# Logarithms of the softmax sums folded into T's rows; the heads' shares applied by ScalarE at O; new step orders

## Chip, cores and metric

One of the eight cores of a Trainium2 chip runs the kernel. The metric is the device time in microseconds. Before the change the median of three runs is 2738.21 us (2737.31 to 2740.78).

## What is computed

A transformer block on 2048 tokens of width 1024. A condition vector gives shifts, scales and gates (`mod`); then a layer norm, attention with 32 heads of width 32 in four segments of 512 tokens, an output projection, a second layer norm and a GEGLU feed-forward of width 3584. In each segment, attention mixes a local softmax with what a memory matrix recalls of the earlier segments:

```python
logits = jnp.einsum("bhqd,bhkd->bhqk", qs, ks) * scale + mask
p = _softmax(logits, axis=-1)
a_dot = jnp.einsum("bhqk,bhkd->bhqd", p, vs)
num = jnp.einsum("bhld,bhde->bhle", pq, M)
den = jnp.einsum("bhld,bhd->bhl", pq, z)[..., None] + 1e-6
a_mem = num / den
o = g * a_mem + (1.0 - g) * a_dot
```

`g` is a sigmoid of `beta`, one number a head.

## The kernel before

All matrix products run on TensorE (PE) with operands split into a high and a low part, three products for one. After an opening (modulation, first layer norm, first projections) comes attention, then the output projection, then the feed-forward by products of half-size blocks.

**Steps.** Attention runs in 32 steps (line 1414): two halves of the sequence, in each eight groups of four heads (g), for each group two segments (s). The loop at line 1605 has three steps in hand: in its turn n the *values* of step n-1 are made, the *scores* of step n, and the *projections* of step n+1. Below, "step n" is turn n of this loop. What a turn does is cut into short pieces with names, and `ORDER` (lines 1415 to 1465) writes out by hand, for each turn, in which order they are issued; every engine and the DMA queue of SyncE (SP) take their instructions strictly in that order. The pieces that matter:

- S0 to S3 (`rows`, line 530): scores with queries as rows. PE makes one S tile a head; VectorE (DVE, line 542) adds the mask and takes the row's maximum with reversed sign into `mm`; ScalarE (ACT, line 544) takes the exponential, and its accumulator gives the row's sum `ll`.
- tm (`maxima`, line 547): DVE splits the maxima into two parts and transposes them in 32x32 blocks. tq (`to_queries`, line 557): DVE writes them into rows 96 to 127 of the query tile `qs`, so that the product T comes out with the maximum subtracted.
- tr (`shares`, line 563): one over the sums, times 1-g (`omg`), on DVE; ACT spreads the factors over 32 columns a head.
- T0 to T3 (line 626): scores again, keys as rows, from the extended queries; ACT takes the exponential (line 633), GpSimd (POOL) masks it (line 634). P0 and P2 (line 638): the products with the values, into the one PSUM tile O.
- rt (`factors`, line 652): PE transposes the spread factors in four blocks into a PSUM tile R (line 649), ACT copies it out. rm (line 656): DVE multiplies O by it. yt (line 659): PE transposes the recalled part Y, DVE adds it. zs stores the result.
- nu, dn, mz: the memory's part; A: this segment's sum for the memory, product M. K0 to K7 and o0, o1 (kn on ACT, vx on DVE): projections to keys and values; kt: keys turned (product kT), copied as kh and kl; dk: three DMAs spread them into `ks`. Q0 to Q3, qo, ea, eb, dq: the same for the queries.
- G, C, D, l, L, m: the next group's weights, fetched, cut on ACT and subtracted on POOL. wl and wd: a row of the modulation, loaded and multiplied on DVE. ns, nc, n, nl: the layer norm of later segments. x, wo, wp, ga: operands of the output projection.

PSUM tiles for S, T, R, Y, M, kT and nu come from one pool of five, taken in turn (`s_ps`, line 99). `sj`, the scores' scratch, has three buffers. The opening (line 1478) sets `omg` at line 1517.

Of the kernel before, what the change touches and what calls it, by code (L numbers as in the profile page):

```python
# [36 lines left out]
def block_kernel(ctx: ExitStack, tc: tile.TileContext, x, c, wmod, wq, wkv, wo, beta, wg, wu, wd, out):  # L37
# [487 lines left out]
    def scores(u, n, g, s):  # L525
# [4 lines left out]
        def rows(i):  # L530
# [7 lines left out]
            for j in range(4):  # L538
# [81 lines left out]
    def values(u, n, g, s):  # L620

        nm = f"{g}_{s}"
        qs, ks, vx = ST[n][:3]
        d, pts = {}, {}

        def T(kc):
            n = L - kc * P
            nn = n
            for j in range(4):
                ps = s_ps(f"T{nm}_{j}{kc}")  # L630
                nc.tensor.matmul(ps[:, :nn], ks[:, j, kc * P:(kc + 1) * P], qs[:, j, L - nn:], start=True, stop=True)  # L631
# [13 lines left out]

        def turned(r, name):
            ps = s_ps(name + nm)
            for i in range(4):
                nc.tensor.transpose(ps[:, i * P:(i + 1) * P], r[:, i].rearrange("p a b -> p (a b)"), ident)  # L649
            return ps  # L650

        def factors():
            d["r"] = tmp_tile("R" + nm)
            nc.scalar.activation(d["r"], turned(SC[n][0], "R"), AF.Copy)

        def scaled():
            nc.vector.tensor_mul(d["r"], d["o"], d["r"])

        def recalled():
            nc.vector.tensor_add(d["r"], d["r"], turned(SY[n], "Y"))  # L660

        for kc in range(4):
            u[f"T{kc}"] = lambda kc=kc: T(kc)
        u["P0"] = lambda: PV(0)
        u["P2"] = lambda: PV(2)
        u["rt"] = factors
        u["rm"] = scaled
        if s > 0:
            u["yt"] = recalled
        u["zs"] = lambda: nc.sync.dma_start(oT_d[g * P:(g + 1) * P, s * L:(s + 1) * L], d["r"])  # L670
# [147 lines left out]
    def feed_forward():  # L818
# [562 lines left out]
        for m in range(NCH):  # L1381
# [96 lines left out]
    def opening():  # L1478
# [244 lines left out]
```

## Time and profile before

| | us |
|---|---|
| median of three runs | 2738.21 |
| the profiled execution | 2737.69 |
| its span, first to last instruction | 2735.9 |
| PE busy | 2710.2 |
| DVE busy | 1553.0 |
| ACT busy | 1202.4 |
| POOL busy | 850.2 |

PE's busy time is nearly the span. A matmul's end is modelled and successive matmuls overlap, so busy time alone doesn't tell whether PE ran at its best: a matmul held back for less than the length of its neighbours shows as a longer distance between starts. In the timeline, rows that repeat are merged: "x4" is four instructions, the first number is the start of the first, the second the time to the end of the last.

### The profile page before, as it was taken

What the parts mean: (1) busy time and instruction counts of PE and PEld (TensorE: products, weight loads), DVE (VectorE), ACT (ScalarE), POOL (GpSimd) and SP (SyncE); (2) the same over time, 40 slices, a digit from 0 to 9 for tenths busy, and PEclk for the clock granted to TensorE, in tenths of its full rate; (3) what the DMA queues carried; (4) which work ended last, traced back from release to release, by engine and by line L of the source; (5) the groups of instructions that cost most, each with busy time, mean ns of one, the idle gap of its engine ahead of it and who ended that gap; (6) DMA issues with size and microseconds to landing.
All of it is one profiled execution on the core that took longest, in us unless ns stands there. A gap on an engine that the chain in (4) does not pass through costs nothing.

```text
span 2735.9 us, 43050 instructions
## 1 busy us (share of the span) xinstructions
PE 2710.2 (99%) x14748; PEld 2279.8 (83%) x14748; DVE 1553.0 (57%) x3516; ACT 1202.4 (44%) x2811; POOL 850.2 (31%) x1446
## 2 busy tenths in 40 slices
PE   7999999999999999999999999999999999999999
PEld 6888888888888888888888888888888888888887
DVE  7777667676777735555555455343433254475456
ACT  6777777667767634343333233111111133233323
POOL 4333334433333434254445451443531000000000
PEclk9999999999999999999999999999999999999999
DMA  7454545444443569788898778999998687795563
GB/s 262 132 147 137 139 122 152 117 117 143 115 129 102 163 211 304 238 300 326 311 351 313 262 276 279 363 359 352 367 353 314 219 316 250 264 306 198 184 207 124
DMA packets 244891, 637.78 MB, mean 233 GB/s; under 512 B 24768, under 2 KB 49344, under 8 KB 244672
## 3 DMA queue, kind: packets, MB, share of 16 engines
q1 hardware_dynamic: 244672, 635.03, 68.2%
q8 instruction: 117, 1.92, 0.3%
q14 instruction: 102, 0.84, 0.1%
HBM read 372.79 MB, written 211.81 MB: 214 GB/s over the span
## 4 chain that ended last, share of the span: by engine, by line
PE 96%; DMA 2%; DVE 1%; issue 0%; ACT 0%; SPq 0%; DVEq 0%; ACTq 0%
PE f L1139 39%; PE y L1353 19%; PE kv L383 12%; PE q L389 6%; PE y L714 5%; PE S L540 3%; PE T L631 3%; PE O L643 3%; PE num L599 1%; PE M L582 1%; PE kv L512 1%; PE tpb L266 1%; PE kT L417 1%; PE R L649 0%; PE Y L649 0%; DMA wm_d<-wmod 0%
## 5 line engine op out<-in xcount | busy, mean ns | idle before, releaser
L1139 PE MATMUL f<-A,B 128*128 128x512 f32 x4704 | 1072.7, 390 | 0.0
L1139 PEld LDWEIGHTS f<-A,B 128*128 128x128 f32 x4704 | 881.4, 188 | 184.4 <-issue 1.0
L1353 PE MATMUL y<-B,L 128*128 128x512 f32 x2352 | 533.3, 389 | 0.0
L1353 PEld LDWEIGHTS y<-B,L 128*128 128x128 f32 x2352 | 441.4, 188 | 91.7
L544 ACT ACTIVATE sj<-sj,mm 128x384 f32<-128x384 f32 (+3 forms) x512 | 281.3, 553 | 49.0 <-DVE mm L542 48.7
L542 DVE CUSTOM_DVE_ANT_0 sj<-S,mask 128x384 f32<-128x384 f32 (+3 forms) x512 | 228.0, 488 | 105.5 <-PE S L540 86.1
L634 POOL TENSOR_SCALAR_AFFINE_SELECT pt<-pt 128x128 f32<-128x128 f32 x512 | 164.1, 343 | 290.0 <-ACT pt L633 283.5
L853 ACT ACTIVATE L<-X 128x512 fp32r<-128x512 f32 x168 | 105.8, 630 | 257.8 <-PE y L1353 166.8
L633 ACT ACTIVATE pt<-T 128x256 f32<-128x256 f32 (+3 forms) x512 | 181.9, 445 | 66.5 <-PE T L631 63.6
L383 PE MATMUL kv<-w,hhh 128*128 128x256 f32 x1024 | 200.3, 286 | 0.0
L855 DVE TENSOR_TENSOR L<-X,L 128x512 fp32r<-128x512 f32 x168 | 115.8, 690 | 146.9 <-ACT L L853 146.7
L1173 ACT ACTIVATE g<-g 128x512 f32<-128x512 f32 x56 | 35.4, 631 | 369.7 <-DVE g L1172 369.7
L374 POOL TENSOR_TENSOR w<-r,w 128x256 fp32r<-128x256 f32 x180 | 134.0, 776 | 158.2 <-ACT w L368 158.1
L383 PE MATMUL kv<-w,hha 128*128 128x256 f32 x896 | 177.2, 285 | 1.9 <-DVE vx L401 1.9
L1078 POOL TENSOR_TENSOR rw<-rw,gbb 128x256 f32<-128x256 f32 x112 | 91.2, 847 | 249.9 <-DMA rw<-wd 167.3
L383 PEld LDWEIGHTS kv<-w,hhh 128*128 128x128 f32 x1024 | 164.8, 191 | 1.4 <-issue 0.4
L383 PEld LDWEIGHTS kv<-w,hha 128*128 128x128 f32 x896 | 144.9, 190 | 4.0 <-DVE vx L401 2.2
L383 PE MATMUL kv<-w,hlh 128*128 128x256 f32 x512 | 144.7, 283 | 0.0
L383 PE MATMUL kv<-w,hla 128*128 128x256 f32 x448 | 126.6, 282 | 0.0
L714 PE MATMUL y<-wo,hho 128*128 128x512 f32 x384 | 126.0, 394 | 0.4 <-DVE xr L718 0.4
L1160 ACT ACTIVATE g<-f 128x512 f32<-128x512 f32 x56 | 33.5, 598 | 206.7 <-PE f L1139 206.7
L1150 ACT ACTIVATE c<-f 128x512 f32<-128x512 f32 x56 | 33.4, 597 | 172.6 <-PE f L1139 172.6
(244 smaller groups left out, 4212.4 us busy)
## 6 DMA issues: line engine op xcount, KB each, us to landing
bc_d<-B SPq DMA_DIRECT2D x189, 512.0 KB, 5.3
B<-bc_d SPq DMA_DIRECT2D x189, 512.0 KB, 5.4
B<-wc_d SPq DMA_DIRECT2D x112, 512.0 KB, 3.7
hid_d<-g SPq DMA_DIRECT2D x56, 512.0 KB, 4.7
wc_d<-T SPq DMA_DIRECT2D x56, 512.0 KB, 7.1
X<-hid_d SPq DMA_DIRECT2D x112, 256.0 KB, 4.7
wr<-gd_d SPq DMA_DIRECT2D x84, 256.0 KB, 4.1
qs<-qh SPq DMA_DIRECT2D x64, 256.0 KB, 3.6
```

Source lines behind the costliest of these rows:

```text
L374: nc.gpsimd.tensor_sub(w[:, 1, c], r[:, c], f32(w[:, 0, c]))
L383: nc.tensor.matmul(ps, b[:, sl], w[:, a], start=(kt == 0 and a == 0 and b is hi), stop=(kt == KT - 1 and a == 1), **kw)
L389: nc.tensor.matmul(ps, w[:, a], b, start=(kt == 0 and a == 0 and b is hi), stop=(kt == KT - 1 and a == 1), **kw)
L542: nc.vector.tensor_tensor_reduce(out=sj[:, :nv], in0=ps[:, :nv], in1=mask[:, L - nv:], scale=-1.0, scalar=3.4e38, op0=ALU.add, op1=ALU.min ...
L544: nc.scalar.activation(sj[:, :nv], sj[:, :nv], AF.Exp, bias=mm[:, j, i:i + 1], scale=-1.0, accum_out=ll[:, i, j:j + 1])
L633: nc.scalar.activation(pt, ps[:, nn - n:nn], AF.Exp)
L634: nc.gpsimd.affine_select(pt[:, :P], pt[:, :P], pattern=[[1, P]], compare_op=ALU.is_ge, fill=0.0, base=0, channel_multiplier=-1)
L714: nc.tensor.matmul(ps, b[:, i * P:(i + 1) * P], w[:, a, g % 2], start=(g == 0 and a == 0 and b is hi), stop=(g == G - 1 and a == 1))
L853: nc.scalar.activation(hi, src, AF.Copy)
L855: eng.tensor_sub(lo[:, k], src[:, k], f32(hi)[:, k])
L1139: nc.tensor.matmul(ps, B[m, i][:, a, kt * P:(kt + 1) * P], A[p, i, kt][b], start=(start and kt == 0 and a == 0 and b == 0), stop=(kt == 3 ...
L1353: nc.tensor.matmul(banks[t], ops[k][:, y, t * P:(t + 1) * P], B[slots[k]][:, x], start=(i not in (2, 4, 3) and j == 0 and x == 0 and y == ...
```

## The change

The row's exponential is divided by its sum in the exponent: the logarithm of the sum is subtracted from the reversed maximum before that goes into the query tile, so that T's exponential gives shares that sum to one. The factors are therefore neither spread, nor transposed, nor multiplied in. tr is now the logarithm on ACT, and stands ahead of tm in every step. 1-g is a column for each group (`omc`), with which ACT scales O at rm. The table set that holds exponential and logarithm is named at the start. rt is gone from all orders, and the orders are written anew. Core of the diff (of the orders, those of which the prediction speaks):

```diff
+    nc.scalar.preload_act_table_set("natural_log_exp_and_others")
...
-    omg = pa.tile([P, H], F32, name="omg")
+    omc = pa.tile([P, G], F32, name="omc")
...
+        def logs():
+            d["ln"] = t2("ln" + nm, "rc", bufs=2, shape=(P, 4, 4))
+            nc.scalar.activation(d["ln"], d["ll"], AF.Ln)
+
         def maxima():
             mm = d["mm"]
+            nc.vector.tensor_sub(mm, mm, d["ln"].rearrange("p i j -> p j i"))
...
-        def shares():
-            rc = t2("rc" + nm, "rc", bufs=2, shape=(P, 4, 4))
-            nc.vector.reciprocal(rc, d["ll"])
-            nc.vector.tensor_mul(rc, rc, omg[:, 4 * g:4 * g + 4].unsqueeze(1).to_broadcast([P, 4, 4]))
-            rx = t2("rx" + nm, "rx", shape=(P, 4, 4, DH))
-            nc.scalar.activation(rx, rc.unsqueeze(3).to_broadcast([P, 4, 4, DH]), AF.Copy)
-            SC[n] = [rx, None]
...
-        u["tr"] = shares
+        u["tr"] = logs
...
-        def factors():
+        def scaled():
             d["r"] = tmp_tile("R" + nm)
-            nc.scalar.activation(d["r"], turned(SC[n][0], "R"), AF.Copy)
-
-        def scaled():
-            nc.vector.tensor_mul(d["r"], d["o"], d["r"])
+            nc.scalar.activation(d["r"], d["o"], AF.Identity, scale=omc[:, g:g + 1])
...
-        u["rt"] = factors
...
         (0,):
-            "N K K N G1 K N N G2 K G0 K S0 S1 C1 S2 K S3 C2 K l1 l2 A tm tr tq L1 K K L2 K",
+            "N K K N G1 K N N G2 K G0 K S0 S1 C1 S2 K S3 C2 K l1 l2 A tr tm tq L1 K K L2 K",
...
         (2, 4, 6, 8):
-            "G1 Q0 T0 wd Q1 T1 Q2 P0 ns nc T2 Q3 T3 qo G2 n0 rt P2 K0 ea eb S0 C1 K1 dq S1 K2 S2 l1 K3 n1 K4 "
-            "nl C2 S3 L1 rm l2 K5 tm G0 wl K6 o0 K7 nd o1 ne tr A tq yt kt dk L2 ek zs",
+            "wd Q0 G2 Q1 Q2 T0 ns Q3 T1 P0 nc T2 A T3 qo n0 K0 nd S0 K1 ea C2 S1 G1 eb dq K2 S2 K3 C1 n1 l2 K4 l1 S3 K5 "
+            "P2 nl o0 L2 tr tm K6 tq rm L1 K7 yt G0 wl o1 kt dk ek zs ne",
...
         (14,):
-            "K0 K1 K2 T0 K3 T1 wd o0 x P0 x T2 S0 x G1 x K4 S1 C1 G2 x A l1 Q0 x S2 L1 Q1 x Q2 S3 x x K5 tm "
-            "T3 Q3 K6 tq K7 qo x P2 o1 C2 l2 rt tr rm G0 yt L2 x x kt ek dq ea dk x zs eb x",
+            "K0 x K1 x Q0 T0 K2 G2 wd T1 K3 S0 wd x x x x P0 o0 x x C2 S1 x l2 Q1 G1 K4 L2 wd Q2 x T2 S2 x x T3 Q3 qo x "
+            "K5 C1 S3 x ea A wd l1 L1 G0 eb K6 dq x K7 P2 o1 tr rm tm kt tq yt ek x dk x x zs x x",
...
         (17,):
-            "D0 K0 K1 K2 mz m0 K3 m1 o0 T0 K4 T1 K5 S0 Q0 S1 K6 S2 P0 T2 Q1 S3 Q2 tm Q3 T3 K7 tq qo P2 o1 rt "
-            "rm yt nu dn dq kt dk tr wl ek ea zs eb",
+            "K0 D0 m0 K1 m1 K2 T0 K3 T1 P0 T2 o0 Q0 T3 wl S0 S1 Q1 S2 Q2 Q3 qo S3 K4 K5 ea K6 K7 P2 mz eb o1 tr rm tm kt "
+            "tq dq yt dk nu dn ek zs",
         (18, 20, 22, 24, 26, 28):
-            "G2 G0 K0 K1 K2 T0 K3 T1 G1 o0 rt P0 T2 Q0 T3 S0 Q1 S1 mz wd Q2 Q3 qo C1 K4 C2 S2 K5 S3 P2 rm l1 "
-            "dq ea yt zs eb K6 K7 A tm nu l2 o1 kt tr ek wl dk tq L1 L2 dn",
+            "K0 G2 K1 K2 T0 mz K3 G1 o0 T1 K4 S0 C2 Q0 S1 P0 S2 Q1 T2 G0 Q2 Q3 wd T3 qo C1 K5 S3 K6 l1 A K7 P2 o1 tr dq "
+            "tm kt L1 rm yt wl ek tq l2 nu dn dk ea eb L2 zs",
         (19, 21, 23, 25, 27):
-            "mz wd D0 K0 K1 K2 m0 m1 K3 o0 T0 K4 T1 Q0 S0 K5 S1 Q1 rt S2 P0 S3 Q2 T2 tm K6 Q3 T3 wl tq qo K7 "
-            "P2 rm o1 nu ea kt yt tr dq dn dk zs wd ek wl eb",
+            "K0 D0 K1 K2 m0 T0 K3 o0 wl T1 K4 S0 Q0 S1 P0 mz m1 wd wd T2 wl Q1 T3 S2 Q2 Q3 qo K5 S3 K6 dq K7 P2 o1 tr tm "
+            "kt tq rm yt nu dk dn ek zs ea eb",
         (29,):
-            "K0 ga K1 D0 mz K2 m0 K3 T0 Q0 wl o0 T1 S0 Q1 S1 P0 S2 K4 S3 tm m1 wo K5 Q2 tq T2 wo Q3 T3 K6 qo "
-            "P2 rt ea eb K7 tr dq rm yt o1 nu dn kt ga dk zs ek",
+            "K0 D0 K1 m0 wd K2 T0 K3 o0 ga T1 K4 S0 K5 wo mz S1 P0 S2 m1 Q0 ga S3 Q1 tr wo tm Q2 T2 Q3 T3 K6 P2 K7 qo ea "
+            "nu tq rm dq o1 yt dn kt eb dk ek wl zs",
...
         (31,):
-            "mz K0 Q0 K1 T0 K2 T1 rt x P0 T2 T3 wp S0 K P2 S1 K K3 K4 S2 Q1 rm K5 S3 tm K6 Q2 tq nu yt K7 Q3 zs tr "
-            "dn",
+            "mz K0 Q0 T0 K1 T1 wp P0 T2 Q1 T3 Q2 S0 K2 K3 P2 S1 K4 rm S2 yt K5 K S3 K K6 tr tm tq nu dn K7 Q3 zs",
...
-        nc.vector.tensor_scalar(omg, gall, -1.0, 1.0, op0=ALU.mult, op1=ALU.add)
+        for j in range(4):
+            q = slice(DH * j, DH * (j + 1))
+            nc.vector.tensor_scalar(omc[q], gall[q].rearrange("p (g j) -> p g j", j=4)[:, :, j], -1.0, 1.0,
+                                    op0=ALU.mult, op1=ALU.add)
```

## Rows read from the trace of the kernel before

**Rows 1.** The page: busy time, share of the span and instructions of each engine.
```profile
PE 2710.2 (99%) x14748; PEld 2279.8 (83%) x14748; DVE 1553.0 (57%) x3516; ACT 1202.4 (44%) x2811; POOL 850.2 (31%) x1446
```

**Rows 2.** Table by stretch, attention: us, busy time, granted clock, DMA share, GB/s.
```profile
80.97:976.00 895.03, 894.01 (x6569) 776.28 (x6568) 621.98 (x2036) 648.10 (x1843) 336.49 (x772) 1.00 0.47 134
```

**Rows 3.** PE's timeline, steps 14, 18, 19, 29: start us, us, engine, line, tiles.
```profile
451.10 2.68 PE L643 MATMUL O<-pt,vx 128*32 128x512 f32 x16
...
563.83 0.86 PE L631 MATMUL T<-qs,ks 128*128 128x384 f32 x4
564.53 0.60 PE L649 MATMUL R<-ident,rx 128*128 128x128 f32 x4
565.06 2.09 PE L643 MATMUL O<-pt,vx 128*32 128x512 f32 x16
...
569.41 0.92 PE L540 MATMUL S<-ks,qs 96*128 96x128 f32 x4
...
596.00 0.56 PE L540 MATMUL S<-ks,qs 96*128 96x128 f32 x4
...
599.75 0.60 PE L649 MATMUL R<-ident,rx 128*128 128x128 f32 x4
600.11 0.95 PE L540 MATMUL S<-ks,qs 96*128 96x384 f32 x4
600.98 1.71 PE L643 MATMUL O<-pt,vx 128*32 128x512 f32 x16
...
873.55 1.36 PE L540 MATMUL S<-ks,qs 96*128 96x128 f32 x4
```

**Rows 4.** Timeline of all engines, end of step 18 to the next T0.
```profile
578.39 1.09 PE L540 MATMUL S<-ks,qs 96*128 96x512 f32 x4
...
583.03 0.19 ACT L544 ACTIVATION_READ_ACCUMULATOR sj<-sj,mm 128x1 f32 x1
...
584.88 0.17 DVE L550 CAST mt<-mm 128x16 fp32r<-128x16 f32 x1
...
585.29 0.86 DVE L555 STREAM_TRANSPOSE tt<-mt 32x32 f32<-32x32 f32 x4
...
587.74 1.70 DVE L559 TENSOR_SCALAR qs<-tt,seli 32x512 fp32r<-32x512 f32 x4
...
591.56 0.63 PE L631 MATMUL T<-qs,ks 128*128 128x512 f32 x2
```

**Rows 5.** Instruction groups by shape, ACT and DVE: xcount | busy us, mean ns | idle.
```profile
L654 ACT ACTIVATE R<-R 128x512 f32<-128x512 f32 x32 | 19.9, 623 | 8.4 <-PE R L649 8.4
...
L334 ACT ACTIVATE h<-tpa,modT 128x512 f32<-128x512 f32 x16 | 12.1, 769 | 6.2 <-DVE modT L171 2.3 <-POOL hla L345 2.3 <-PE tpa L327 1.4
...
L127 ACT ACT_TABLE_LOAD x1 | 1.3, 1283 | 0.8 <-PEq L1716 0.8
L1160 ACT ACT_TABLE_LOAD x1 | 1.3, 1283 | 0.0
...
L127 ACT ACTIVATE gall<-bb 128x32 f32<-128x32 f32 x1 | 0.2, 229 | 1.8 <-DMA bb<-beta 1.8
...
L657 DVE TENSOR_TENSOR R<-O,R 128x512 f32<-128x512 f32 x32 | 21.9, 686 | 3.3 <-PE O L643 2.8 <-ACT R L654 0.4
```

**Rows 6.** DVE's timeline in the opening; idle time and its releaser in brackets.
```profile
8.84 0.69 DVE L232 BATCH_NORM_STATS2 sta<-x 128x6 f32<-128x512 f32 x1 [0.74 <-DMA x<-x]
```

**Rows 7.** The chain of waits, in order of time: start us, us, what.
```profile
585.97 5.75 PE kv L383 x48
```

**Rows 8.** DVE's timeline, end of step 0.
```profile
75.83 3.09 DVE L559 TENSOR_SCALAR qs<-tt,seli 32x512 fp32r<-32x512 f32 x4
```

**Rows 9.** Timelines of ACT and POOL behind T1 of step 18.
```profile
564.26 1.64 ACT L633 ACTIVATE pt<-T 128x384 f32<-128x384 f32 x4 [0.23 <-PE T L631]
...
564.82 1.44 POOL L634 TENSOR_SCALAR_AFFINE_SELECT pt<-pt 128x128 f32<-128x128 f32 x4 [0.43 <-ACT pt L633]
```

**Rows 10.** The page, DMA issues: xcount, KB each, median us from issue to landing.
```profile
qs<-qh SPq DMA_DIRECT2D x64, 256.0 KB, 3.6
```

More of the change, by code (lines that the diff above doesn't have):

```diff
@@ L348, in norm_seg @@
             yield
-    hT, W, Mst, ST, SC, SY, PK = {}, {}, {}, {}, {}, {}, {}
+    hT, W, Mst, ST, SY, PK = {}, {}, {}, {}, {}, {}
     ks_t = []
@@ L1416, in block_kernel @@
         (0,):
-            "N K K N G1 K N N G2 K G0 K S0 S1 C1 S2 K S3 C2 K l1 l2 A tm tr tq L1 K K L2 K",
+            "N K K N G1 K N N G2 K G0 K S0 S1 C1 S2 K S3 C2 K l1 l2 A tr tm tq L1 K K L2 K",
         (1,):
-            "K0 T0 K1 D0 ns K2 T1 rt nc P0 mz m0 nu dn K3 T2 n0 n1 o0 Q0 Q1 T3 nd S0 ne nl m1 P2 S1 rm S2 K4 "
-            "Q2 S3 yt tm Q3 K5 K6 K7 tq wl qo o1 zs tr dq A kt ea eb dk ek",
+            "T0 K0 mz K1 T1 A P0 T2 ns K2 K3 nc D0 T3 n0 K4 nd n1 o0 K5 S0 m0 Q0 S1 K6 S2 m1 Q1 S3 Q2 Q3 nu dn ne nl K7 "
@@ L1421, in block_kernel @@
+            "qo tr P2 o1 rm ea tm tq kt dq dk yt eb zs ek",
         (2, 4, 6, 8):
-            "G1 Q0 T0 wd Q1 T1 Q2 P0 ns nc T2 Q3 T3 qo G2 n0 rt P2 K0 ea eb S0 C1 K1 dq S1 K2 S2 l1 K3 n1 K4 "
-            "nl C2 S3 L1 rm l2 K5 tm G0 wl K6 o0 K7 nd o1 ne tr A tq yt kt dk L2 ek zs",
+            "wd Q0 G2 Q1 Q2 T0 ns Q3 T1 P0 nc T2 A T3 qo n0 K0 nd S0 K1 ea C2 S1 G1 eb dq K2 S2 K3 C1 n1 l2 K4 l1 S3 K5 "
+            "P2 nl o0 L2 tr tm K6 tq rm L1 K7 yt G0 wl o1 kt dk ek zs ne",
         (3, 5, 7):
-            "ns D0 K0 K1 T0 K2 T1 nc m0 K3 wl o0 wd P0 n0 K4 S0 K5 S1 mz Q0 S2 Q1 A S3 nd K6 m1 n1 tm nl Q2 "
@@ L1426, in block_kernel @@
-            "tq rt T2 Q3 ne T3 qo ea K7 P2 o1 rm nu dq tr dn yt kt dk eb zs ek",
+            "mz D0 K0 K1 m0 T0 K2 T1 K3 ns m1 P0 nc T2 wl o0 n0 Q0 S0 K4 A S1 Q1 S2 K5 S3 n1 Q2 K6 nl Q3 tr wd T3 tm qo "
+            "tq K7 P2 o1 nu ea nd dq rm ne eb yt kt dn dk zs ek",
         (9,):
-            "D0 K0 K1 m0 T0 K2 T1 mz K3 P0 T2 Q0 o0 S0 Q1 m1 S1 K4 S2 Q2 Q3 T3 qo K5 S3 K6 K7 tm A P2 tq o1 "
-            "dq ea kt dk rt tr rm yt nu dn wd ek wl eb zs",
+            "K0 D0 K1 m0 T0 K2 T1 m1 K3 P0 T2 Q0 o0 S0 Q1 S1 Q2 S2 K4 Q3 T3 K5 qo S3 mz tr ea K6 tm K7 P2 o1 A rm eb kt "
@@ L1430, in block_kernel @@
+            "nu dq tq yt dn ek dk zs",
         (10, 12):
-            "G2 K0 K1 G1 K2 rt T0 K3 o0 T1 G0 K4 S0 Q0 S1 C1 l1 Q1 L1 S2 P0 wd Q2 S3 K5 Q3 T2 K6 wl tm tq T3 "
-            "K7 qo A dq ea C2 P2 o1 tr rm kt yt l2 ek eb dk zs L2",
+            "K0 wl wd K1 K2 G1 T0 K3 o0 T1 K4 S0 P0 wd T2 S1 Q0 S2 Q1 S3 Q2 tr Q3 G0 wl tm T3 K5 qo ea tq C1 K6 l1 K7 G2 "
+            "P2 o1 A L1 rm dq yt C2 kt ek dk l2 eb L2 zs wl",
         (11, 13):
-            "K0 T0 D0 K1 T1 m0 rt wl m1 K2 P0 T2 K3 wd T3 Q0 mz o0 S0 Q1 S1 wl Q2 S2 K4 A Q3 qo S3 K5 dq tm "
@@ L1435, in block_kernel @@
-            "K6 K7 P2 rm tq o1 kt yt nu tr ea zs dk dn ek wd eb",
+            "T0 K0 D0 A T1 K1 P0 m0 T2 K2 Q0 wd S0 Q1 m1 S1 K3 o0 Q2 T3 S2 Q3 qo K4 dq S3 mz K5 K6 tr tm ea K7 tq P2 o1 "
+            "rm yt zs kt nu dn ek eb dk",
         (14,):
-            "K0 K1 K2 T0 K3 T1 wd o0 x P0 x T2 S0 x G1 x K4 S1 C1 G2 x A l1 Q0 x S2 L1 Q1 x Q2 S3 x x K5 tm "
-            "T3 Q3 K6 tq K7 qo x P2 o1 C2 l2 rt tr rm G0 yt L2 x x kt ek dq ea dk x zs eb x",
+            "K0 x K1 x Q0 T0 K2 G2 wd T1 K3 S0 wd x x x x P0 o0 x x C2 S1 x l2 Q1 G1 K4 L2 wd Q2 x T2 S2 x x T3 Q3 qo x "
@@ L1439, in block_kernel @@
+            "K5 C1 S3 x ea A wd l1 L1 G0 eb K6 dq x K7 P2 o1 tr rm tm kt tq yt ek x dk x x zs x x",
         (15,):
-            "K0 wd T0 rt T1 K1 D0 m0 P0 T2 m1 K2 mz x T3 A wd S0 K3 x o0 x S1 Q0 Q1 S2 K4 S3 Q2 tm x Q3 nu "
-            "K5 K6 x qo K7 tr wd P2 ea x eb x tq o1 dn x x rm kt wl ek dq dk wd x yt x zs x",
+            "D0 K0 m0 K1 m1 K2 T0 K3 o0 T1 K4 S0 Q0 S1 Q1 S2 mz Q2 x S3 A tr Q3 P0 x T2 tm K5 T3 nu K6 K7 wl tq qo ea P2 "
+            "o1 x eb wl rm dn x wd kt dq yt dk zs ek",
@@ L1442, in block_kernel @@
         (16,):
-            "Q0 G1 K0 T0 mz Q1 T1 Q2 P0 T2 Q3 T3 qo G2 C1 rt dq K1 ea S0 eb C2 P2 l1 K2 rm S1 yt K3 S2 K4 S3 "
-            "K5 o0 K6 K7 zs tm o1 l2 L1 nu A kt tr tq L2 G0 dk ek dn",
+            "K0 G1 wd T0 mz x Q0 T1 A P0 x T2 Q1 T3 G2 Q2 S0 K1 S1 Q3 S2 K2 K3 o0 qo ea C2 C1 S3 tr P2 l2 G0 rm l1 eb K4 "
+            "K5 K6 tm dq K7 o1 nu tq yt L2 dn kt L1 ek dk zs",
         (17,):
-            "D0 K0 K1 K2 mz m0 K3 m1 o0 T0 K4 T1 K5 S0 Q0 S1 K6 S2 P0 T2 Q1 S3 Q2 tm Q3 T3 K7 tq qo P2 o1 rt "
@@ L1456, in block_kernel @@
-            "P2 rt ea eb K7 tr dq rm yt o1 nu dn kt ga dk zs ek",
+            "K0 D0 K1 m0 wd K2 T0 K3 o0 ga T1 K4 S0 K5 wo mz S1 P0 S2 m1 Q0 ga S3 Q1 tr wo tm Q2 T2 Q3 T3 K6 P2 K7 qo ea "
+            "nu tq rm dq o1 yt dn kt eb dk ek wl zs",
         (30,):
-            "ga wp K0 x mz T0 K1 wp K2 T1 K3 o0 x K4 S0 x K5 x S1 Q0 S2 x wl x wo Q1 x Q2 x S3 K6 P0 x T2 Q3 "
-            "T3 tm wo tq K7 qo P2 dq o1 x rt wp rm yt kt wd dk nu x ea eb tr dn A x ek zs",
+            "mz K0 ga x x T0 K1 T1 wp wp K2 K3 wl wl P0 o0 S0 K4 S1 Q0 S2 Q1 x wo x S3 x wo x Q2 K5 tr x K6 T2 K7 T3 wp "
@@ L1460, in block_kernel @@
+            "Q3 tm tq nu qo P2 x ea o1 dq eb rm yt dn A x kt dk x x x x zs ek",
         (31,):
-            "mz K0 Q0 K1 T0 K2 T1 rt x P0 T2 T3 wp S0 K P2 S1 K K3 K4 S2 Q1 rm K5 S3 tm K6 Q2 tq nu yt K7 Q3 zs tr "
-            "dn",
+            "mz K0 Q0 T0 K1 T1 wp P0 T2 Q1 T3 Q2 S0 K2 K3 P2 S1 K4 rm S2 yt K5 K S3 K K6 tr tm tq nu dn K7 Q3 zs",
         (32,):
-            "K0 K1 Q0 K2 T0 K3 T1 rt P0 T2 Q1 T3 K4 K5 Q2 P2 rm yt K6 zs K7 Q3",
+            "K0 Q0 K1 K2 T0 Q1 T1 K3 Q2 P0 T2 Q3 T3 K4 K5 K6 P2 rm yt zs K7",
```

## The prediction

> **What bounds the kernel now.** I read the busy shares first. TensorE (PE) is busy for 2710.2 of 2735.9 us [rows 1]. The table by stretch says the same of attention: from 80.97 to 976.00 us, where every step of the changed order lies, PE is busy for 894.01 of 895.03 us, at a granted clock of 1.00, the 2.4 GHz level, while VectorE (DVE), ScalarE (ACT) and GpSimd (POOL) have 622, 648 and 336 us of work [rows 2]. So time goes only where PE's own stream gets shorter, or where it pauses. The pauses are not shown as idle, because a matmul that waits is merged with its neighbours; they are seen in PE's timeline, by comparing equal groups [rows 3]. The four S0 matmuls take 0.92 us at 569.41 and 0.56 us at 596.00; the O group takes 2.09 us at 565.06 and 1.71 us at 600.98. The differences, 0.36 and 0.38 us, are waits. Last I read DVE and ACT between the last S of a step and the first T of the next [rows 4], the chain that the change lengthens.
>
> **Step by step, what the change removes.** (1) *The R transposes.* Each of 32 steps loses four transposes and their PSUM tile; 128 of them. What a group costs PE is the distance to the next group's start: 0.36 us from 599.75 to 600.11, 0.53 us from 564.53 to 565.06 [rows 3]. All 32 at one or the other give 11.5 or 17.0 us; in PE's timeline 13 are of the 0.53 kind, 12 of the 0.36 kind, 7 lie between 0.38 and 0.81. I take 14.6 us. All of it is on PE, so nothing covers it and all of it is gained, unless a pause takes its place.
>
> (2) *DVE and ACT work.* Per step DVE loses the multiply with R (0.686 us) and two operations on 16 columns; it gains one on 16 columns, a subtraction, for which the cast of the same size stands (0.17). ACT loses the copy of R (0.623) and the spreading of the factors over as many columns; it gains a logarithm of 16 columns (the exponential of 32 columns took 0.229) and the scaling of O [rows 4, 5]. No row shows ACT scaling O by a column: a copy from PSUM (0.623) and the scale-and-bias operation with two columns (0.769) bound it; I take 0.70, between them. Both engines end up with less work, about 0.7 and 0.3 us a step, at no direct gain, as PE covers both.
>
> (3) *The opening.* Four column operations replace the one that made omg: three more of about 0.17 us on DVE. DVE then stands idle for 0.74 us until x lands [rows 6], which swallows 0.5 us: I cost it at nothing; without that cover it is 0.5 us.
>
> **What it adds: the logarithm in the chain.** Today the maxima go straight to their transposes; the sums are needed only by tr. After the change tm, on DVE, waits for the logarithm, the logarithm for the last exponential of S3, and then tq, and the next step's T0, follow. Behind tm on DVE's queue stand kl, the addition of Y, tq and vx in some orders; PE waits for none of them before kT and T0. I lay step 18's new tail out from S3's start, by rows. PE needs 13.2 us from S3 to the next T0 today (578.39 to 591.56). The changed order has the same groups between them but for K3, a quarter of the 5.75 us that K0 to K3 take in the chain of waits [rows 7], and without the 0.3 us in which they paused; that leaves about 11.4 us. Today ACT's last accumulator of S3 is read 4.8 us after S3's start (578.39 to 583.22) [rows 4]. Then kn 0.4 and logarithm 0.23: 5.5. DVE: vx, subtraction 0.17, cast to transposes 1.27 (584.88 to 586.15): 7.2. Then kl and the addition of Y, 1.25: 8.45. Then tq: 1.70 us in this step [rows 4], but 3.09 us at 75.83, where the same four operations ran slower [rows 8]. So tq ends at 10.2 to 11.6 us against T0 at 11.4: between 1.2 us early and 0.2 us late. I cost the chain at nothing, near its early end, because today's equal place ran at 1.70.
>
> **What the new orders move.** Gains: in the six even steps 18 to 28 S0 no longer follows T3 nor O the T1 and R groups: K4 or S0, Q0 and S1 stand between. I count both waits as gone: 6 x (0.36 + 0.38) = 4.4 us. In step 14 O took 2.68 us, in step 29 S0 1.36 [rows 3]: by the same comparison 1.0 and 0.8 us, and there too K groups now stand between. Together 6.2 us; at the least nothing of it.
> Losses: steps 2, 4, 6, 8, 17 and 31 now issue P0 right behind T1. T1 began at 563.83 [rows 3]; its exponentials ended at 565.90 and POOL's four masks at 566.26 [rows 9], 2.43 us after. The fourth head is needed about half-way into O, 0.9 us, so P0 can start 1.5 us after T1 unhindered, but T1 lasts 0.70: 0.85 us of waiting, 5.1 us in six steps. In the odd steps 19 to 27 kT stands right behind P2, 4.6 us after S3's start, while kn waits behind S3's exponentials on ACT's queue until 5.1: 0.5 us, 2.5 us in five. Together 7.6 us; at the least 0, and at the most again as much.
> DMAs: dk comes after kl, 7.8 us after S3; with its issue and a landing like qs's 3.6 us [rows 10] the keys are there at about 12.5, and S0 of the next step comes at 15.9. The weights' fetches, wl, zs and dq keep whole K groups ahead of those who need them on SP's queue. POOL's weight differences (l1 to L2) move to the step's end, where POOL idles until the next T0. I cost these at nothing; if SP or POOL were late, S0 or O would pause.
>
> **Tables.** In the trace ACT loads a table twice, 1.283 us each, at the first exponential and at the first Gelu, and never between [rows 5]. The preload takes the place of the first, so I add nothing.
> The Trainium skill (ScalarE: Activation LUTs, "Table sets: the hidden batching unit") says that exponential and logarithm need one load only if the set that holds both is active, and charges about 2.7 us for each switch otherwise. By that rule the sum is the same with the named set, and 32 x 2 x 2.7 = 173 us of ACT time, an estimate from that page, without it; no run so far shows a logarithm.
>
> **Sum.** -14.6 - 6.2 + 7.6 = -13.2 us on a profiled execution of 2737.7 us (span 2735.9), 0.5 us below the median of 2738.2 shown. Taken from the median: 2725 us, a ratio of 0.995.
>
> **Rivals.** *A, the waits that the orders are to remove go, and no new ones come.* -14.6 - 6.2: 2717 us. For it: ACT and DVE have less work, and one PSUM tile a step less is asked for. Against: P0 directly behind T1. *B, half or more of the gain is lost to new pauses:* R at its lower bound, 11.5, no old wait gained, and the 7.6 us of new ones: 2734; with R as forecast 2731. For it: today's groups are already spaced so that most pauses are under 0.4 us, so little can be won back.
> *C, T0 waits for tq in every step (slower than before).* The place is tq behind tm on DVE; the price is what the chain is longer than my layout, less the 1.2 us of slack, times 31 steps. It decides the sign at 1.2 + 13.2/31 = 1.6 us a step. The slow tq brings 1.4 of it, and an ACT one accumulator late another 0.7; then 2.1 - 1.2 = 0.9 us a step, 28 us: 2753. Against it: today's T0 came 2.1 us after tq had ended (589.43 to 591.56) [rows 4], with K0 to K3 between, one K group more than now.
> *D, the set is not kept, so each step loads tables twice:* the first load stands in the chain, 1.28 us, just over its slack, and the second falls before the next T's exponentials and can hold O back by as much: 32 x 1.28 = 41 us at most, 2766; none if both find ACT idle. Against: ACT's only two loads today stand where the functions change.
>
> **Chances.** Forecast, 2719 to 2731: 0.62. A: 0.10. B: 0.16. C: 0.08. D: 0.04. About 0.2% (5.5 us) is what a measurement of this kernel can tell from no change. Faster: forecast, A and half of B, 0.80. Within it: half of B and part of D, 0.11. Slower: C and the rest of D, 0.09. The range reaches from A with R near its upper bound, 2714 (-17.0 - 6.2, and a microsecond for pauses not listed), to B's end and a microsecond more, 2735; it leaves out C, D and a few hundredths of B.
>
> **What would show it.** Right: no matmul at R; 128 fewer on PE; from S3 to the next T0 in step 18 about 11.4 us; S0 at 0.56 us and O at 1.71 in the even steps; tq ending before T0; two table loads. P0 behind T1 at about 2.6 us instead of 1.7 in step 2. Wrong: T0 starting at tq's end in most steps (C), a table load before each logarithm (D), O and kT groups that grew by more than 0.85 and 0.5 us (B).

## The result and the profile after

The changed kernel takes 2743.56 us (median of 20 runs, 2738.26 to 2746.33), the kernel before 2739.74 us beside it: a ratio of 1.0014, 95% interval 1.0007 to 1.0020. Forecast were 2725 us, 13.2 us faster than before; it is 3.8 us slower, a small loss that the interval still tells from none. The profiled execution took 2743.34 us with a span of 2741.5.

The page's busy shares, against [rows 1]:

```profile
PE 2706.3 (99%) x14620; PEld 2270.8 (83%) x14620; DVE 1545.3 (56%) x3455; ACT 1191.4 (43%) x2811; POOL 843.6 (31%) x1446
```

128 matmuls are gone, as the diff says, and DVE, ACT and POOL have less work than before. The table by stretch, for the stretch of [rows 2]:

```profile
80.97:976.00 895.03, 884.57 (x6430) 762.73 (x6430) 610.81 (x1980) 639.11 (x1844) 333.24 (x772) 1.00 0.48 135
```

PE is now idle for 10.5 us of this stretch, where it was idle for 1.0. Two pauses, of 4.42 and 3.57 us, lie across its two ends; 4.8 us of them fall inside it. The rest is many small waits, of which more below. The view of PE's waits (engine, line waited for: us in total, times, longest) names them, first around 70 to 90 us, then from 960 us on:

```profile
PE T L629 <- DVE qs L565: 4.4, 1, 4.4
...
PE O L641 <- POOL pt L632: 3.6, 1, 3.6
```

**The first, end of step 0.** Timelines of ACT, DVE, POOL and PE (start us, us, engine, line, tiles; in brackets the idle time before it and its releaser):

```profile
75.96 1.04 ACT L369 ACTIVATE w<-r 128x1024 fp32r<-128x1024 f32 x1
76.91 0.20 ACT L550 ACTIVATE ln<-ll 128x16 f32<-128x16 f32 x1
...
77.14 0.71 DVE L554 TENSOR_TENSOR mm<-mm,ln 128x16 f32<-128x16 f32 x1 [1.83 <-ACT ln L550]
77.88 0.63 DVE L556 CAST mt<-mm 128x16 fp32r<-128x16 f32 x1
...
80.13 2.36 DVE L565 TENSOR_SCALAR qs<-tt,seli 32x512 fp32r<-32x512 f32 x4
...
77.08 4.32 POOL L375 TENSOR_TENSOR w<-r,w 128x256 fp32r<-128x256 f32 x6 [4.74 <-ACT w L369]
...
82.55 2.07 PE L629 MATMUL T<-qs,ks 128*128 128x512 f32 x4 [4.42 <-DVE qs L565]
```

The logarithm takes 0.20 us, but it stands behind the cut of the next weights (C2, 1.04 us) on ACT, and DVE waits 1.83 us for it. It ends just as POOL begins its differences, and DVE runs slower beside them: the cast takes 0.63 us, where the same cast took 0.17 at 584.88 [rows 4]. In the kernel before, the tail began without the logarithm, and K0 stood ahead of T0. Now T0 is first in step 1, and PE stands still for 4.42 us. The kernel before paused here too, for 0.87 and 1.93 us; in the second pause K0 waited for vx, which on DVE's queue stands behind tq:

```profile
76.79 0.71 PE L417 MATMUL kT<-ident,kn 128*128 128x128 f32 x4 [0.87 <-ACT kn L400]
79.43 0.38 PE L383 MATMUL kv<-w,hha 128*128 128x256 f32 x1 [1.93 <-DVE vx L401]
```

**The second, step 32:**

```profile
969.79 1.06 ACT L189 ACTIVATE wo<-ro 128x1024 fp32r<-128x1024 f32 x1 [2.58 <-DVE ro L685]
970.76 0.76 ACT L631 ACTIVATE pt<-T 128x128 f32<-128x128 f32 x4
...
970.94 5.09 POOL L194 TENSOR_TENSOR wo<-ro,wo 128x256 fp32r<-128x256 f32 x4 [3.37 <-ACT wo L189]
975.98 1.02 POOL L632 TENSOR_SCALAR_AFFINE_SELECT pt<-pt 128x128 f32<-128x128 f32 x4
...
972.11 0.64 PE L641 MATMUL O<-pt,vx 128*32 128x256 f32 x8
976.33 1.37 PE L641 MATMUL O<-pt,vx 128*32 128x128 f32 x8 [3.57 <-POOL pt L632]
```

The output's weights are fetched, split on ACT and subtracted on POOL bit by bit: each projection group that is issued also issues a piece of this side work. The new order has eight groups ahead of T3, the old one six. So the weights' split comes ahead of T3's exponentials on ACT, their differences (5.09 us) ahead of T3's masks on POOL, and P2 waits for the masks.

**Both pauses cost a second time.** The table by stretch, columns as in [rows 2]; the granted clock is the third from the end:

```profile
38.14:44.96 6.82, 6.82 (x30) 6.43 (x30) 5.71 (x18) 6.01 (x10) 5.97 (x10) 0.50 0.25 97
...
79.10:82.51 3.41, 0.00 (x0) 0.00 (x0) 3.28 (x9) 1.16 (x3) 2.30 (x4) 1.00 0.62 156
82.51:85.92 3.41, 3.37 (x12) 2.99 (x13) 3.33 (x7) 2.06 (x4) 1.50 (x5) 0.50 0.22 77
973.40:976.80 3.40, 0.47 (x4) 0.28 (x4) 1.36 (x1) 1.84 (x2) 3.40 (x7) 1.00 0.15 54
976.80:980.21 3.41, 3.41 (x14) 2.60 (x13) 0.69 (x1) 0.69 (x1) 3.41 (x6) 0.50 0.23 77
```

Behind each of the two stretches in which PE did next to nothing the granted clock is 0.50, the 1.2 GHz level, for 3.41 us, in which PE does half of what it could: 1.7 us lost each time. The opening has such a stretch in both kernels, of 3.41 us before and of 6.82 us here (first row). That one is not the change's: two runs below with the changed kernel's opening have 3.41 us there (e14) and none (e7). So one profiled execution can differ from another by some 3 us, and prices are taken from medians or from the length of a step.

**The rest.** The pair of steps 18 and 19 takes 54.72 us from T0 to T0, 55.80 before. Steps 2, 4, 6, 8 and 17 have P0 behind T1, and O takes 0.82 us longer there than the 1.64 us that its group needs elsewhere; in 16 it is 0.78, in 31 even 1.45. The pair 10 and 11 got 1.17 us longer (56.00 for 54.83), the pair 12 and 13 1.50 (55.95 for 54.45). From T0 of step 10 to T0 of step 18 it is 226.0 us, where it was 222.8. Three of the new waits in PE's timeline, in steps 11, 14 and 29:

```profile
369.28 0.91 PE L580 MATMUL M<-vx,pk 128*128 128x130 f32 x6 [0.66 <-DVE pk L432]
...
466.92 1.34 PE L541 MATMUL S<-ks,qs 96*128 96x384 f32 x4
...
881.57 1.50 PE L541 MATMUL S<-ks,qs 96*128 96x512 f32 x4
```

S2 took 0.88 us in step 14 before (at 459.59), and S3 takes 1.09 in step 18 [rows 4].

### The profile page after: what moved, and what is told of

It is laid out like the page before. It is cut to its first block, busy times and chain, and to the rows that moved or that the text cites. A ratio compares the mean times of both kernels' runs of the same rounds, so it can differ in the third digit from the quotient of the medians.

```text
span 2741.5 us, 42690 instructions
## 1 busy us (share of the span) xinstructions
PE 2706.3 (99%) x14620; PEld 2270.8 (83%) x14620; DVE 1545.3 (56%) x3455; ACT 1191.4 (43%) x2811; POOL 843.6 (31%) x1446
## 4 chain that ended last, share of the span: by engine, by line
PE 91%; DVE 3%; DMA 2%; ACT 1%; issue 1%; POOL 1%; SPq 0%; DVEq 0%; ACTq 0%; POOLq 0%
PE f L1133 38%; PE y L1347 19%; PE kv L384 11%; PE q L390 6%; PE y L708 5%; PE S L541 3%; PE T L629 3%; PE O L641 3%; DVE qs L565 1%; ACT sj L545 1%; PE M L580 1%; PE kv L513 1%; PE num L597 1%; PE tpb L267 0%; PE kT L418 0%
## 5 line engine op out<-in xcount | busy, mean ns | idle before, releaser
L543 DVE CUSTOM_DVE_ANT_0 sj<-S,mask 128x384 f32<-128x384 f32 (+3 forms) x512 | 226.0, 488 | 90.4 <-PE S L541 65.7
L629 PE MATMUL T<-qs,ks 128*128 128x256 f32 (+3 forms) x512 | 108.0, 330 | 6.4 <-DVE qs L565 4.4
```

The lines of the kernel that those rows point to most:

```text
L543: nc.vector.tensor_tensor_reduce(out=sj[:, :nv], in0=ps[:, :nv], in1=mask[:, L - nv:], scale=-1.0, scalar=3.4e38, op0=ALU.add, op1=ALU.min ...
```

## The experiments

Each ran beside the kernel before on the same chip; medians in us. Runs that show the same time for before shared a chip; across chips the ratios are the better comparison.

| run | this | before | ratio, 95% interval |
|---|---|---|---|
| changed kernel | 2743.56 | 2739.74 | 1.0014, 1.0007 to 1.0020 |
| e6 old orders | 2749.05 | 2739.45 | 1.0034, 1.0021 to 1.0047 |
| e7 no logarithm | 2737.80 | 2739.45 | 0.9993, 0.9984 to 1.0002 |
| e1 step 32 | 2737.66 | 2739.45 | 0.9991, 0.9983 to 1.0000 |
| e2 steps 0, 1 | 2739.19 | 2739.45 | 0.9998, 0.9989 to 1.0007 |
| e8 old orders, no logarithm | 2733.85 | 2741.06 | 0.9979, 0.9970 to 0.9988 |
| e9 before, no R | 2732.25 | 2741.06 | 0.9973, 0.9964 to 0.9982 |
| e10 before, R of one transpose | 2733.53 | 2741.06 | 0.9975, 0.9966 to 0.9984 |
| e5 all repairs | 2733.62 | 2741.06 | 0.9976, 0.9966 to 0.9986 |
| e13 old orders, O scaled by DVE | 2748.53 | 2740.16 | 1.0029, 1.0018 to 1.0041 |
| e11 three repairs | 2731.84 | 2740.16 | 0.9968, 0.9956 to 0.9981 |
| e12 four repairs | 2730.36 | 2740.16 | 0.9964, 0.9952 to 0.9977 |
| e14 filler | 2744.97 | 2739.60 | 1.0019, 1.0010 to 1.0028 |

My theory at the start, P: R's 14.6 us are there, and a few places of the new orders eat them. Rival L: the logarithm costs something in every step. Rival N: R stood where PE waits anyway.

**e1, step 32 alone.**

```diff
-(32,) "K0 Q0 K1 K2 T0 Q1 T1 K3 Q2 P0 T2 Q3 T3 K4 K5 K6 P2 rm yt zs K7"
+(32,) "K0 K1 Q0 K2 T0 K3 T1 P0 T2 Q1 T3 K4 K5 Q2 P2 rm yt K6 zs K7 Q3"
```

> The changed kernel with the order of step 32 alone put back to that of before (without rt): six projection groups ahead of T3 in place of eight, so that the fetched weights' split on ScalarE and its differences on GpSimd stand behind T3's exponentials and masks. Theory P: P2's wait of 4.7 us goes to about 1 us, and the half-clock stretch at 976.8 (3.4 us, so 1.7 lost) goes with it: -3.8 - 1.7 = -5.5 us, 2738. Rival (the pause only moves to another group of this step): no change, 2743 to 2744.

5.9 us less than the changed kernel, as expected. In its trace the split and the differences are behind T3's work, and P2 runs through:

```profile
966.34 0.88 ACT L631 ACTIVATE pt<-T 128x128 f32<-128x128 f32 x4 [0.59 <-PE T L629]
973.93 1.06 ACT L189 ACTIVATE wo<-ro 128x1024 fp32r<-128x1024 f32 x1 [6.71 <-DVE ro L685]
...
966.68 1.03 POOL L632 TENSOR_SCALAR_AFFINE_SELECT pt<-pt 128x128 f32<-128x128 f32 x4 [0.58 <-ACT pt L631]
975.08 1.44 POOL L194 TENSOR_TENSOR wo<-ro,wo 128x256 fp32r<-128x256 f32 x2 [7.36 <-ACT wo L189]
...
970.66 0.86 PE L641 MATMUL O<-pt,vx 128*32 128x256 f32 x16
```

No stretch at half clock is left there. The cause of the second pause is shown.

**e2, steps 0 and 1.**

```diff
-(0,) "... S0 S1 C1 S2 K S3 C2 K l1 l2 A tr tm tq L1 K K L2 K"
+(0,) "... S0 S1 C1 l1 L1 S2 K S3 K A tr C2 tm K K tq l2 L2 K"
-(1,) "T0 K0 mz K1 T1 ..."
+(1,) "K0 T0 mz K1 T1 ..."
```

> The changed kernel with steps 0 and 1 rearranged: C2 behind the logarithm on ScalarE, GpSimd's l1 ahead of the tail and not in it, one projection group between tm and tq, and K0 ahead of T0 in step 1. Theory P: T0's wait for tq of 4.4 us goes to under 1 us, and the half-clock stretch at 82.5 (1.7 lost) with it: -3 to -5 us, 2739 to 2741. Rival (K0 then waits for vx behind tq, as it did for 1.9 us in the kernel before, and the rest moves to S0): -1 us or nothing, 2742 to 2744.

4.4 us less. PE's waits there:

```profile
PE T L629 <- DVE qs L565: 1.5, 1, 1.5
```

T0 still waits 1.5 us where I expected under 1, since tq, at 2.79 us beside POOL, stays slow; but no half-clock stretch follows.

**e7, the price of the logarithm in the new orders.**

```diff
-            nc.vector.tensor_sub(mm, mm, d["ln"].rearrange("p i j -> p j i"))
```

> The changed kernel without the subtraction of the logarithms from the maxima (left out: the division by the sums; tm then waits for the last maximum alone, and the logarithm is still computed). It prices the wait for the logarithm in all steps at once. Theory P: only the steps whose tq ends just before T0 gain (0, 10 to 14): 2 to 5 us, so 2738 to 2742. Rival L: 32 steps x 0.5 us or more, 16 us, so 2727 or less.

5.8 us less, a little over the 5 us that P allowed at most, far under L's 16. In the trace nearly all of it is at one place: from kT of step 0 to kT of step 1 it takes 30.41 us, where the changed kernel took 34.75. Every later step has its length within 0.4 us, and 10 to 13 within 0.02, which I had listed as steps that pay. In the new orders the logarithm is thus paid for in step 0, and there for the place where it stands.

**e6, the new arithmetic in the old orders.** All orders are those of before; rt is taken out and tr put directly ahead of tm.

```diff
-(18, ...) "... o0 rt P0 T2 ... A tm nu l2 o1 kt tr ek wl dk tq ..."
+(18, ...) "... o0 P0 T2 ... A tr tm nu l2 o1 kt ek wl dk tq ..."
```

> The new arithmetic in the orders of the kernel before: rt is taken out, tr stands directly ahead of tm, nothing else moves. Theory P (the gain of the R transposes, 14.6 us, is there, and a few places in the new orders eat it): no new pause of the new orders can be here, the old waits stay, so about -14.6 plus at most 4 us for the steps whose tq was near to T0: 2723 to 2730, about 2726. Rival L (the logarithm in the chain costs something in every step): 2735 to 2750. Rival N (the transposes lay in time that PE would wait anyway): 2736 to 2742.

2749.05, slower than before and than the changed kernel: P falls. A few places of the new orders are not all that eats R's gain; without these orders the loss is larger. So I asked for the parts of this loss.

**e8, e9 and e10: R and the logarithm apart.** e8 is e6 without the subtraction. e9 and e10 change the kernel before:

```diff
 e9: rt out of all orders;  e10: rt kept, with one transpose and a copy of 128 columns
-            nc.vector.tensor_mul(d["r"], d["o"], d["r"])
+            nc.vector.tensor_copy(d["r"], d["o"])
```

> The new arithmetic in the orders of before, without the subtraction of the logarithms (left out: the division by the sums). Theory N (R stood where TensorE waits anyway, so its 14.6 us do not come, and the rest of the 9.6 us by which the run with the old orders is slower than before is the wait for the logarithm in steps 0, 1, 30 and 32): 2737 to 2741. Rival P (R's gain is there and the logarithm eats it everywhere): 2725. Rival M (the loss is neither, but the removed PSUM tile or the scaling on ScalarE): 2745 to 2749.

> The kernel before without the four R transposes, their PSUM tile and their copy; rm copies O on VectorE in the place of the product (left out: the heads' shares and the division by the sums). Nothing else is changed, no logarithm. Theory N: the pauses behind R grow by what R took: 2736 to 2741, no gain. Rival P: R's 14.6 us come out: 2723 to 2727.

> The kernel before with one R transpose in place of four, and a copy of its 128 columns; rm copies O (left out as in the run without R). The PSUM tile stays in its place in the ring of tiles, so that every later group gets the buffer that it had. Theory N by cover (what stands behind R waits for exponentials and masks): as the run without R, 2736 to 2741. Rival ring (R's gain is lost because without its tile T0 gets the buffer that num still holds, 0.43 us in every odd step): 3/4 of R's 14.6 us come out here and not there: 2727 to 2730.

All three came between the theories. Without R the kernel before gains 8.8 us by the medians (4.9 to 9.9 by the interval), not 14.6 and not nothing. e10, which keeps R's place in the ring of PSUM tiles, gains 7.5, so the ring is not where the rest went. Where it went is seen by groups. PE's timeline of e9 in step 18, against 563.83 to 565.06 in [rows 3]:

```profile
561.16 0.86 PE L631 MATMUL T<-qs,ks 128*128 128x384 f32 x4
561.95 2.53 PE L643 MATMUL O<-pt,vx 128*32 128x512 f32 x16
564.41 0.74 PE L631 MATMUL T<-qs,ks 128*128 128x256 f32 x4
```

With R between them O took 2.09 us, without it 2.53: O starts 0.44 us sooner behind T1 and spends these 0.44 us waiting for T1's exponentials and masks, and the step takes 30.10 us, as before (30.09). So it is in all even steps 18 to 28, in 31 and in 32, and nearly so in 2 to 8 (29.35 for 29.44). Where R stood between groups that wait for nothing, it is gained: the odd steps 19 to 27 take 25.27 us for 25.71. (In this profiled execution step 15 takes 32.31 us for 30.24: PE pauses 0.77 and 1.02 us there, and from 474.01 on the granted clock is 0.50 for 3.41 us.)

e8 against e7 sets the old orders against the new ones, both without the logarithm: 0.9979 for 0.9993, so there the old orders are 3.8 us ahead, with intervals that just overlap. The new orders too seem to eat some of R's gain, step 32 above all (5.9 us, e1); they are the better ones only with the logarithm. e8 against e6 is the logarithm in the old orders: by the ratios 0.55%, 15 us. PE's waits of e6, then of e8:

```profile
PE kv L384 <- DVE vx L402: 8.2, 6, 4.9
PE y L708 <- DVE pq L461: 2.4, 1, 2.4
```

```profile
PE kv L384 <- DVE vx L402: 1.5, 1, 1.5
PE y L707 <- DVE pq L461: 0.8, 1, 0.8
```

PE does not wait for tq, which the prediction watched, but for what stands behind tm and tq on DVE's queue: vx in step 1, pq in step 30. There, ACT's and DVE's timelines of e6:

```profile
926.27 0.24 ACT L550 ACTIVATE ln<-ll 128x16 f32<-128x16 f32 x1
...
926.54 0.25 DVE L554 TENSOR_TENSOR mm<-mm,ln 128x16 f32<-128x16 f32 x1 [3.13 <-ACT ln L550]
```

DVE stands for 3.13 us, because the logarithm comes behind T3's exponentials on ACT. These waits are 8.3 us of the 15; a half-clock stretch of 6.83 us from 83.19 on, which e8 does not have, makes another 3.4.

**e13, O scaled by DVE in the old orders.**

```diff
-            nc.scalar.activation(d["r"], d["o"], AF.Identity, scale=omc[:, g:g + 1])
+            nc.vector.tensor_scalar(d["r"], d["o"], omc[:, g:g + 1], None, op0=ALU.mult)
```

> The new arithmetic in the orders of before (2749 us), with O scaled by VectorE as the product with R was, in place of ScalarE; the logarithm stays. It asks what of the loss there is rm's move to ScalarE, where it stands behind S3's exponentials and holds VectorE's addition of Y, and with it tm and tq. By the steps' lengths of the two kernels without R and without the logarithm, which differ in nothing else: 0.5 us in each odd step 19 to 27, 1 us in 11 and 13, 1.1 us in 30: 5 to 6 us. Theory: 2742 to 2745. Rival (the logarithm alone, which waits for the same exponentials, holds tm as long): 2747 to 2750.

0.5 us less than e6 (1.4 by the ratios), within the spread: the rival holds. Moving rm to ScalarE is not a cost of its own where the logarithm holds tm anyway.

**e14, R's work put back where P0 waits.** Four transposes that nobody reads:

```diff
-(2, 4, 6, 8) "... T1 P0 nc T2 ..."
+(2, 4, 6, 8) "... T1 fl P0 nc T2 ..."
```

> The changed kernel with four transposes of the identity put between T1 and P0 in steps 2, 4, 6, 8, 17 and 31, in a PSUM tile that nobody reads: the work of R, added where P0 waits today (O 0.82 us over its 1.64 in 2 to 8). Theory N (R stood in the shadow of the exponentials and masks before P0): the steps keep their lengths, 27.26 us in step 2, O's excess falls to about 0.4, and the time stays at 2743 to 2744. Rival P (each R group costs TensorE what it takes): step 2 at 27.6 to 27.8 us, and 6 x (0.36 to 0.53) = 2.2 to 3.2 us in all: 2746 to 2747.

PE's timeline in step 2, the changed kernel first, then e14:

```profile
119.04 0.86 PE L629 MATMUL T<-qs,ks 128*128 128x384 f32 x4
119.83 2.53 PE L641 MATMUL O<-pt,vx 128*32 128x512 f32 x16
122.28 0.74 PE L629 MATMUL T<-qs,ks 128*128 128x256 f32 x4
```

```profile
118.58 0.86 PE L629 MATMUL T<-qs,ks 128*128 128x384 f32 x4
119.28 0.60 PE L657 MATMUL F<-ident 128*128 128x128 f32 x4
119.81 2.08 PE L641 MATMUL O<-pt,vx 128*32 128x512 f32 x16
121.82 0.74 PE L629 MATMUL T<-qs,ks 128*128 128x256 f32 x4
```

From T1 to T2 it is 3.24 us in both: four more transposes cost nothing, in step 2 and, within 0.04 us of a step's length, in each of the other five (step 2 takes 27.27 us for 27.26). N is shown for these places. The median is 1.4 us higher, within both intervals; the profiled execution has longer half-clock stretches behind the two pauses, and one more later.

**e5, e11 and e12: repairs together.** e5 takes e1 and e2, puts a projection group between T1 and P0 in 2, 4, 6, 8, 17 and 31, and changes 10 to 13. e11 leaves 10 to 13 out. e12 adds, to e11:

```diff
-(11, 13) "T0 K0 D0 A T1 K1 P0 m0 T2 K2 Q0 ..."
+(11, 13) "K0 T0 D0 K1 T1 K2 P0 m0 T2 A Q0 ..."
```

> The changed kernel with the repairs of steps 0, 1 and 32 of the two runs before, and with one projection group put between T1 and P0 in steps 2, 4, 6, 8, 17 and 31, between T2 and S1 in 10 and 12, and K0 ahead of T0 in 11 and 13. Theory (the pauses of the new orders can be taken out one by one): -5.9 - 4.4 as measured, -0.82 x 6 = -4.9 for P0 and -2 to -4 for 10 to 13: 2725 to 2729. Rival (the pauses behind P0 only move to the next group): 2732 to 2734.

> The run with all repairs without the ones of steps 10 to 13 (these keep the changed kernel's orders). By the steps' lengths in that run's trace the repair of 10 and 12 made the pair 10/11 0.84 us longer (56.84 for 56.00), and so did 12/13. Theory (pauses add up by the steps in which they stand): 1.7 us less than the run with all: 2731 to 2733. Rival (what a step wins the next gives back): as the run with all, 2733 to 2735.

> The run before this one, and in steps 11 and 13 K0 ahead of T0, K2 between T1 and P0, and A behind T2, against T0's wait of 0.65 us and A's of 0.83. Theory: both waits go: -1.5 us in each of two steps, 2728 to 2730. Rival (S0 or O then waits for the exponentials of T2 in their place, as O did for 1.23 us in the run with all): 2731 to 2734.

e5 came out at its rival. The pieces ahead of P0 won little: 2 and 3 take 56.03 us for 56.65, but 4 and 5, 6 and 7 only 56.39, for there O still waits 0.51. And e5's orders of 10 and 12 have one group fewer behind S3, so that the K0 that follows kT waits 1.44 us for vx, which stands behind tq on DVE. Without that part e11 gains 1.8 us, as its theory said. In e12 the waits of T0 and A in 11 and 13 are gone (steps 10 to 13 take 109.63 us for 111.93, 2.3 less; by the medians it is 1.5). Its stretch of attention:

```profile
80.97:976.00 895.03, 889.57 (x6474) 767.73 (x6474) 610.48 (x1977) 640.29 (x1845) 342.26 (x781) 1.00 0.48 136
```

PE idles for 5.5 us of it instead of 10.5. At 0.9964 e12 beats both kernels, with the change's arithmetic kept.

## Why the prediction was wrong

The sum said -13.2 us; +3.8 came, a miss of 17.0. The experiments divide it, by their ratios, into three parts. R gone in the old orders, without the logarithm (e8): -5.8 us, where -14.6 were forecast. The new orders in place of the old, still without it (e7 against e8): +3.8, where the old waits and the losses were to make +1.4. The logarithm in the new orders (the changed kernel against e7): +5.8, where 0 was forecast. By the intervals each part is good to 2 or 3 us. The division goes by way of the old orders; how much R costs in the new ones was tried in six steps only (e14).

**The R transposes, -14.6 us: mis-sized.** The step that failed is "All of it is on PE, so nothing covers it and all of it is gained, unless a pause takes its place". I priced a group by its distance to the next one's start. That is worth what I said only if the next group is free to start. In the old orders it was not in twelve steps, where O, behind R, waits for exponentials and masks: e9 gives 8.8 us. e14 shows the same in the new orders: behind T1, where P0 waits, R's work goes back for nothing. The row was there: [rows 3] show O at 2.09 us behind R, 0.38 over its 1.71 elsewhere, a sign that O was waiting for something that R covered in part. In the even steps 18 to 28 the new orders put other groups ahead of O; there R's time was gained.

**New waits in steps 10 to 16: not in the sum.** From T0 of step 10 to T0 of step 18 the sum makes 3.4 us less (R in seven steps 3.2, step 14 1.0, against 0.85 in step 17); 3.2 us more came. Of the losses there I had listed P0 in step 17 alone. In 11 and 13 T0 waits 0.67 us and A 0.84, in 10 and 12 S1 0.64, and e12 wins 2.3 us in these four steps. In 14 to 16 the waits are only read from the trace; no run takes them away. Hardly any of this is the logarithm's: in e7 these steps keep their lengths within 0.3 us.

**The chain, 0 us: wrong by 5.8 us in these orders.** In step 18 the layout holds: tq ended 11.39 us after S3's start and T0 came at 11.71, where I had 10.2 to 11.6 and 11.4. But I laid out one step and costed 32 by it. In step 0 ACT has C2's cut ahead of the logarithm, DVE is slowed by POOL, and T0 lost K0. Rival C named the mechanism and was wrong in its extent: one step, not 31. In the old orders the chain would have cost 15 us (e6, e8); much of what the new orders do is to bring this to 5.8. The prediction does not say so anywhere. One sentence of its layout is wrong too: that PE waits before T0 for none of what stands behind tm on DVE. The kernel before has K0 waiting 1.93 us for vx there (79.43), and in e6 it is 4.9 us.

**The side work of step 32: not in the sum.** "I cost these at nothing; if SP or POOL were late, S0 or O would pause." O did: P2's group took 5.5 us, 4.7 over the 0.8 of other steps. The projection groups were counted as PE's cover, not as what each issues on ACT and POOL. With the half clock it made 5.9 us (e1).

**Right, in part or whole.** *Old waits, -6.2.* In the six even steps 18 to 28 S0 and O no longer wait: 0.56 and 1.71 us in step 20. These two, with R of both steps (0.53 and 0.36), are 1.63 us a pair; 1.08 came. Most of the difference is a new wait of 0.44 us, T0's fourth head in the odd steps, for ry to leave its PSUM buffer. I had expected one of 0.5 us at kT, which does not wait; that the sum of a pair came out so near (-1.13 forecast) is luck. In steps 14 and 29, 1.8 of the 6.2 us, S0 and O are free as forecast, but others wait in their place: 1.6 us in step 14 (a Q group, S2 and T3), 0.9 in step 29 (T0 and S3), about as much as was won. *P0 behind T1*: 0.85 us forecast, 0.82 measured in five of the six steps, 1.45 in step 31. *D*: the rows of ACT:

```profile
L652 ACT ACTIVATE R<-O,omc 128x512 f32<-128x512 f32 x32 | 21.8, 682 | 8.1 <-PE O L641 8.1
L550 ACT ACTIVATE ln<-ll 128x16 f32<-128x16 f32 x32 | 6.7, 208 | 0.4
L117 ACT ACT_TABLE_LOAD x1 | 1.3, 1283 | 0.8 <-PEq L1712 0.8
L1154 ACT ACT_TABLE_LOAD x1 | 1.3, 1283 | 0.0
```

The scaling takes 0.68 us (0.70 forecast) and the logarithm 0.21 (0.23). Two tables are loaded, as before, and none before a logarithm, as the rule in the Trainium skill (ScalarE: Activation LUTs, "Table sets: the hidden batching unit") says of a set that holds both functions.

**What stays open.** The sum is not closed to the microsecond: e12 is 9.8 us under before, and I forecast 13. S1 behind T2 in 10 and 12 (0.64 us each), a Q group that waits 1.1 us for vx in step 15, T0 behind ry in the odd steps, and P0 in 4 to 8 and 16 are still there; orders that remove them were not tried.

## What to carry to other kernels

Before you count a removed group as gained, look at what stands behind it: if that group waits for another engine, the removed one was its cover, and its time comes back as the wait. A chain that gets longer is laid out at its worst step, with what stands ahead of each link on that step's queues, not at a typical one; and when a group is moved, whatever side work its call brings along moves with it.

## What was not expected of the hardware

A long pause is paid for twice: behind 4.42 and 3.57 us in which PE stood still, the granted clock was 0.50 for 3.41 us (in e14 for 6.83 us, behind pauses of 4.41 and 4.43 us in the same places), and where a repair took the pause away, that stretch went too. Shorter pauses did it too, as in e9 two of 0.77 and 1.02 us close together, while a single one of 1.46 us in e2 and the two of 0.87 and 1.93 us in the kernel before did not. What decides is not shown here.

VectorE's small operations took longer while POOL subtracted weights: the cast of 16 columns 0.63 us for 0.17, tq 2.36 us in step 0 and 3.56 in steps 10 and 12 for 1.69, and the new subtraction 0.71 us in step 0, where the median of its 32 is 0.19. They lie on the chain that this change lengthens, so that its length depends on where POOL's work is put. The Trainium skill (SBUF — State Buffer, "Who interferes with whom") says that the two engines share one pair of ports, that a VectorE instruction with two inputs in SBUF, or one in a two-port mode, contends there with GpSimd, and that the one that is first holds the pair for its whole instruction while the other is blocked. That agrees in kind: in e2, where POOL begins only after them, the subtraction and the cast of step 0 take 0.19 and 0.18 us. No run here took POOL's work away alone.
